# Attention products moved to even slots and input loads spaced out, in a fused attention and gated-MLP kernel

## The chip, the cores and the metric

One core of a Trainium2 chip. The metric is the device time of one launch in microseconds; a ratio is the mean time of one kernel's runs over the mean of the other's runs of the same rounds, so it is not quite the ratio of the medians quoted beside it. Each job runs the kernel before on the same chip beside the new ones.

## The reference, cut to what matters

```python
batch, n_heads, seq, head_dim = (8, 8, 576, 64)          # fp32 q, k, v

def _attn_ref(q, k, v, tau):
    scores = scale * np.matmul(q, k.transpose(0, 1, 3, 2))
    thresh = np.max(scores, axis=-1, keepdims=True) - tau
    scores = np.where(scores >= thresh, scores, -1000000000.0)
    attn = np.exp(scores - np.max(scores, axis=-1, keepdims=True))
    attn = attn / (np.sum(attn, axis=-1, keepdims=True) + 1e-09)
    return np.matmul(attn, v)

def _moe_ref(x, w_in, w_out):                            # x: 4608 x 512, w_in: 512 x 2048
    h = x @ w_in
    return ((h * np.clip(h + 3.0, 0.0, 6.0) / 6.0) @ w_out)
```

The heads of one image (batch entry) are put side by side to make the rows of `x`.

## The kernel before: the parts that matter here

The loop has 144 slots, nine per "quad" (four heads of one image, two pairs). A slot handles 128 query rows of two heads: score matmuls, the maximum on VectorE, mask and exp on ScalarE, the normalisation on GpSimd (L319), then a DMA transpose of the bf16 row, 128 x 1152 (L327), issued from SyncE. Slots 0 to 3 of a quad are its first pair, 4 to 7 its second, slot 8 is the remainder (64 rows of each of the four heads). Once a pair's rows are transposed, the attention product (`av_main`, L343) multiplies them by v; `av_rest` does the remainder. When an image is complete, its gate/up products (`mm1`, L378) are put on a list that gives one item to a slot, and its output products (`mm2`, L412) on another that gives two parts to an even slot. What is left of both lists is done behind the loop, in the tail. Four buffers hold normalised rows until their transposes have read them. From slot 22 on, rows are normalised, and their transposes issued, two at a time in odd slots. Inputs are loaded as fp32; from image 2 on q and k are loaded in 32-column blocks (four DMAs per group), and VectorE transposes the 32x32 blocks.

```python
    nat_pool = ctx.enter_context(tc.tile_pool(name="nat", bufs=3))
    v_pool = ...; qk_pool = ...; s_pool = ...          # cut
    pn_pool = ctx.enter_context(tc.tile_pool(name="pn", bufs=4))
    # ... cut ...
        def blocks_q(n, a, j):
            c = 32 * (2 * a + j)
            nc.sync.dma_start(out=nq[c:c + 32, n * S:(n + 1) * S].rearrange("p (k d) -> p k d", d=32),
                              in_=q[b, 4 * g + 2 * n + a, :, 32 * j:32 * j + 32].rearrange("(k r) d -> r k d", r=32))

        # blocks_k: the same for k; load_k(n) and load_q(n) issue four of them for the heads 2n and 2n+1 ... cut ...

        def rest():
            for dst, src in ((kr[:], k), (nq[:, 1024:1152], q))[0:2 if b < NB else 1]:
                for n in range(2):
                    nc.sync.dma_start(out=dst[64 * n:64 * n + 64, :].rearrange("p (h d) -> p h d", h=2),
                                      in_=src[b, 4 * g + 2 * n:4 * g + 2 * n + 2, 512:S, :].rearrange("h p d -> p h d"))

        for n in range(2):
            loads.append(lambda n=n: load_k(n))
            loads.append(lambda n=n: load_q(n))
            if n == 0:
                loads.append(rest)

    def sm_norm(sl):
        sl.pn = pn = pn_pool.tile([P, 2, S], BF16, tag="pn", name="pn")
        for i in range(2):
            nc.gpsimd.tensor_scalar(out=pn[:, i, :], in0=sl.s[:, i, :], scalar1=sl.rinv[:, i:i + 1], scalar2=1.0,
                                    op0=Alu.mult, op1=Alu.mult)
        if sl.slot < 8:
            pair, t = 2 * sl.quad + sl.slot // 4, sl.slot % 4
            sl.dst = pts[pair][:, :, t * P:(t + 1) * P]
        else:
            sl.dst = ptr[sl.quad][:, :, :]
        if not sl.on_chip:
            nc.sync.dma_start_transpose(out=sl.dst, in_=pn[:].rearrange("p a b -> p (a b)"))

    def av_main(pair):
        b, hp = divmod(pair, NPAIR)
        if hp == 0:
            xT[b] = x_pool.tile([P, KI, 512], BF16, tag="xT", name="xT")
        pb = bank()
        av(pb, pair, pts[pair], slice(0, 512))
        return lambda: nc.vector.tensor_copy(out=xT[b][:, hp, :], in_=pb)

    for n, sl in enumerate(queue):
        quad, slot = sl.quad, sl.slot
        b, g = divmod(quad, 2)
        now = n
        # ... cut: allocation, load_quad(quad + 2) at slot 0 of a quad (quad 5's at slot 4 of quad 3, n = 31), load_v(b + 1) at slot 0 of an odd quad ...
        # ... cut: exp of the slot before, scores' maximum of the slot after ...
        if todo1:
            item, then = todo1.pop(0)
            h = mm1(item)
            r = mm1_relu(h, on_act=even)
            mm1_gate(item, h, r)
            todo2.extend(then)
        copies = pe_transpose(queue[n - 2]) if n > 1 and queue[n - 2].on_chip else None
        if prev is not None and n < N1:
            sm_recip(prev)
        if copies:
            copies()
        for _ in range(2 if n % 2 == 0 and todo2 else 0):
            bb, mt, part = todo2.pop(0)
            mm2_part(bb, mt, part)
        for i in range(2):
            sm_mask(sl, i)
        if slot == 3 and quad > 0:
            waiting.append(av_main(2 * quad - 1))
        elif slot == 4 and quad > 0:
            waiting.append(av_rest(quad - 1))
            if quad % 2 == 0:
                todo1.extend(moe_of(quad // 2 - 1))
        if slot == 8:
            waiting.append(av_main(2 * quad))
        # ... cut: output of mm2; copies out of PSUM, put off by one slot in even slots ...
        evict = []
        for job, of in turns.get(n, ()):
            if job == "k":
                evict.append(transpose_k(of))
            elif job == "q":
                if of // 2 not in qkT:
                    alloc_qk(of // 2)
                evict.append(transpose_q(of))
            else:
                (last_keys if even else evict).append(transpose_rest(of, of_k=of > 0))
        # ... cut: scores of later slots (two slots' worth in odd slots) ...
        if prev is not None:
            ready.append(prev)
        if not even:
            for old in ready:
                sm_norm(old)
            ready = []
        flush()
        if n == 0:
            start(loads, 2)
        elif n not in (4, 12, 15, 18, 21) and not 23 < n < 34:
            start(loads, 1)
        if n < 4 or 15 < n < 20 or n > 33:
            start(vcasts, 1)
        else:
            start(casts, 2 if n in (5, 8, 11, 14) or 21 < n < 28 else 1)
        prev = sl
```

All DMA issues above, except those of v, which GpSimd issues, stand in SyncE's one queue, in the order of the program.

Of the kernel before, what the change touches and what calls it, by code (L numbers as in the profile page):

```python
# [20 lines left out]
def kernel(  # L21
# [17 lines left out]
    NQUAD = B * H // 4  # L39
    NSLOT = 9  # L40
    NB = 2
# [34 lines left out]
    loads = []  # L76
# [5 lines left out]
    def load_quad(quad):  # L82
        b, g = divmod(quad, 2)
        nat[quad] = (nat_pool.tile([P, 1152], F32, tag="nq", name="nq"),
                     nat_pool.tile([P, 4, 4, D], F32, tag="km", name="km"),
                     nat_pool.tile([P, 2 * D], F32, tag="kr", name="kr"))
        nq, km, kr = nat[quad]

        def main(dst, src, h, order, by=nc.sync):
            by.dma_start(out=dst[:, :, h, :], in_=src[b, 4 * g + h, 0:512, :].rearrange(order, t=4))  # L90
# [6 lines that stand above are left out]
        def blocks_k(n, a, j):  # L97
            c = 32 * (2 * a + j)
            nc.sync.dma_start(
                out=km[c:c + 32].rearrange("p t h d -> p (t h d)")[:, n * 512:(n + 1) * 512].rearrange(  # L100
                    "p (t m d) -> p t m d", t=4, d=32),
                in_=k[b, 4 * g + 2 * n + a, 0:512, 32 * j:32 * j + 32].rearrange("(m r t) d -> r t m d", r=32, t=4))

        def load_k(n):
            if b < NB:
                for a in range(2):
                    main(km, k, 2 * n + a, "(p t) d -> p t d")
            else:
                for a in range(2):
                    for j in range(2):  # L110
                        blocks_k(n, a, j)

        def load_q(n):
            if b < NB:
                for a in range(2):
                    main(nq[:, 0:1024].rearrange("p (t h d) -> p t h d", h=4, t=4), q, 2 * n + a, "(t p) d -> p t d",
                         by=nc.scalar if quad == n == 0 else nc.sync)
            else:
                for a in range(2):
                    for j in range(2):  # L120
                        blocks_q(n, a, j)
# [4 lines that stand above are left out]
                    nc.sync.dma_start(out=dst[64 * n:64 * n + 64, :].rearrange("p (h d) -> p h d", h=2),  # L126
                                      in_=src[b, 4 * g + 2 * n:4 * g + 2 * n + 2, 512:S, :].rearrange("h p d -> p h d"))

        for n in range(2):
            loads.append(lambda n=n: load_k(n))  # L130
            loads.append(lambda n=n: load_q(n))
            if n == 0:
                loads.append(rest)

    def load_v(b):
        vm = v_pool.tile([P, H, 4 * D], BF16, tag="vm", name="vm")
# [72 lines left out]
    def bank():  # L209
        nonlocal turn  # L210
        turn += 1
        return ps[:, (2, 5)[turn % 2], :]
# [135 lines left out]
# [8 lines that stand above are left out]
    def av_rest(quad):  # L356
# [3 lines that stand above are left out]
            av(pb[:, n * 64:(n + 1) * 64], 2 * quad + n, ptr[quad], slice(n * 64, (n + 1) * 64))  # L360
        if b % 2 == 0 and g == 0:
            xR[b // 2] = x_pool.tile([P, KI, P], BF16, tag="xR", name="xR")
        o0 = 64 * (b % 2)
        return lambda: nc.vector.tensor_copy(out=xR[b // 2][:, 2 * g:2 * g + 2, o0:o0 + 64],
                                             in_=pb[:, 0:P].rearrange("p (a b) -> p a b", a=2))
# [61 lines left out]
    todo1 = []  # L427
# [52 lines left out]
    def turn_at(n, job, of):  # L480
        turns.setdefault(n, []).append((job, of))

    for quad in range(1, NQUAD):
        n0 = quad * NSLOT
        first_odd = n0 - 9 + quad % 2
        for i, (job, of) in enumerate((("q", 2 * quad), ("k", 2 * quad), ("rest", quad),
                                       ("q", 2 * quad + 1), ("k", 2 * quad + 1))):
            turn_at(n0 + (-5, -4, -3, 0, 1)[i] if quad < 3 else first_odd + 2 * i - (job == "rest"), job, of)

    prev = None  # L490
    ready = []
    last_keys = []
    part = 0
    waiting = []
# [4 lines that stand above are left out]
        if slot in (0, 4):  # L499
            pts[2 * quad + slot // 4] = pt_pool.tile([P, 9, 512], BF16, tag="pT", name="pT")  # L500
        if slot == 8:
            ptr[quad] = ptr_pool.tile([P, 9, P], BF16, tag="pR", name="pR")
        for ahead in {0: (1, 2), 9: (3,), 16: (4,)}.get(n, (quad + 2,) if quad > 2 and slot == (4 if quad == 3 else 0) else ()):
            if ahead < NQUAD:
                load_quad(ahead)
        if slot == 0 and g == 1 and b + 1 < B:
            load_v(b + 1)
        for copy in last_keys:
            copy()
        last_keys = []  # L510
        if prev is not None:
            for i in range(2):
                sm_exp(prev, i)
        if n + 1 < len(queue):
            sm_max(queue[n + 1])
        even = n >= N1 and n % 2 == 0
        for old in ready:
            sm_recip(old)
        for copy in waiting:
            copy()  # L520
        waiting = []
# [14 lines that stand above are left out]
            mm2_part(bb, mt, part)  # L536
        for i in range(2):
            sm_mask(sl, i)
        if slot == 3 and quad > 0:
            waiting.append(av_main(2 * quad - 1))  # L540
        elif slot == 4 and quad > 0:
            waiting.append(av_rest(quad - 1))
            if quad % 2 == 0:
                todo1.extend(moe_of(quad // 2 - 1))
        if slot == 8:
            waiting.append(av_main(2 * quad))
        if part == 3:
            waiting.append(lambda tile=(bb, mt): late.extend(mm2_out(*tile, on_act=False)))
            part = 0
        if n < N1 or n % 2:  # L550
            for copy in waiting:
                copy()
            waiting = []
# [10 lines that stand above are left out]
        if n >= N1 and not even:  # L564
            sm_recip(prev)
        for out_of_psum in evict:
            if out_of_psum:
                out_of_psum()
        if n == 0:
            warm_up(8)  # L570
        if n <= N1:
            scores(n + 2)
        elif n % 2:
            for m in (n + 3, n + 2):
                if m < len(queue):
                    scores(m)
        if n < 8:
            warm_up(6)
# [6 lines that stand above are left out]
        flush()  # L585
        if n == 0:
            start(loads, 2)
        elif n not in (4, 12, 15, 18, 21) and not 23 < n < 34:
            start(loads, 1)
        if n < 4 or 15 < n < 20 or n > 33:  # L590
            start(vcasts, 1)
# [3 lines that stand above are left out]
# [80 lines left out]
```

## Time and profile before

| | |
|---|---|
| time, median of 3 runs | 563.53 us |
| profiled span | 562.4 us |
| PE / ScalarE / VectorE / GpSimd busy | 93% / 81% / 78% / 49% |
| from the start of slot 36 to that of slot 54 (quads 4 and 5) | 73.5 us |
| an undisturbed pair of quads (10 and 11) | 61.2 us |
| last masks to the end (tail) | 61.5 us |

A stretch is cut at the start of the first mask (a ScalarE instruction of L306, two a slot) of a quad's first slot. The lines that carry this, and how to read them, stand in the prediction.

### The profile page before, as it was taken

How to read it: one execution, taken by the hardware profiler on the slowest of the kernel's cores; microseconds unless marked ns; L12 is line 12 of the kernel's file. 1: busy time of each engine (PE TensorE's matmuls, PEld its weight loads, DVE VectorE, ACT ScalarE, POOL GpSimd, SP SyncE). 2: the span in 40 equal slices, each digit the busy share in tenths (PEclk: the TensorE clock that was granted, in tenths of full speed). 3: DMA queues.
4: the chain of work that ended last, by engine and by line, in shares of the span. 5: the costliest groups of instructions: out<-in, count | busy, mean ns of one | idle time of the engine just before them, and what ended most of it. 6: DMA issues, size and time to landing. Idle time of an engine off the chain costs nothing.

```text
span 562.4 us, 11583 instructions
## 1 busy us (share of the span) xinstructions
PE 520.9 (93%) x3823; PEld 323.4 (58%) x3865; DVE 439.0 (78%) x1093; ACT 455.5 (81%) x983; POOL 278.2 (49%) x502
## 2 busy tenths in 40 slices
PE   8999988997975899999999899999999999999996
PEld 6765555664543565666556565666555566664662
DVE  3888878895894798989898698988898889872540
ACT  3999979997884799899898699898898899891540
POOL 1788877564444444644465344745465454550000
PEclk9999999998997999999999899999999999999999
DMA  5899999878899878999889979999889966662302
GB/s 121 135 163 151 164 132 182 139 108 158 146 148 175 141 144 138 158 156 178 144 160 179 171 118 163 145 153 167 147 163 176 170 105 119 110 120 82 76 20 75
DMA packets 316589, 78.74 MB, mean 140 GB/s; under 512 B 299504, under 2 KB 312048, under 8 KB 316528
## 3 DMA queue, kind: packets, MB, share of 16 engines
q1 hardware_dynamic: 297920, 68.69, 69.0%
q0 software_dynamic: 17408, 8.92, 13.7%
q8 instruction: 30, 0.49, 0.4%
q10 hardware_dynamic: 1200, 0.39, 0.3%
q14 instruction: 31, 0.25, 0.2%
HBM read 36.70 MB, written 9.44 MB: 82 GB/s over the span
## 4 chain that ended last, share of the span: by engine, by line
PE 52%; ACT 9%; DMA 6%; DVE 4%; issue 3%; POOL 2%; SPq 1%; DVEq 0%; POOLq 0%; ACTq 0%
PE ps L284 17%; PE ps L412 15%; PE ps L378 13%; DMA pT<-pn 6%; PE ps L343 5%; ACT s L311 4%; ACT s L306 3%; PE ps L373 2%; POOL pn L319 1%; ACT r L386 1%; DVE s L299 1%; PE ps L346 1%; DVE g L401 1%; ACT kT L219 1%; DMA nq<-in_q_dram 0%
## 5 line engine op out<-in xcount | busy, mean ns | idle before, releaser
L319 POOL TENSOR_SCALAR pn<-s,rinv 128x576 bf16<-128x576 f32 x288 | 211.1, 745 | 83.9 <-issue 46.1
L299 DVE TENSOR_SCALAR_CACHE_REDUCE s<-ps 128x576 f32<-128x576 f32 x288 | 205.8, 752 | 40.0 <-PE ps L284 19.8
L306 ACT ACTIVATE s<-s,bias 128x576 f32<-128x576 f32 x288 | 205.8, 763 | 9.2 <-POOL bias L302 8.9
L311 ACT ACTIVATE s<-s 128x576 f32<-128x576 f32 x288 | 192.4, 670 | 0.3
L284 PE MATMUL ps<-kT,qT 64*128 64x384 f32 (+7 forms) x1280 | 186.5, 425 | 3.4 <-DVE s L299 1.6
L284 PEld LDWEIGHTS ps<-kT,qT 64*128 64x128 f32 (+1 forms) x1280 | 117.6, 178 | 60.0 <-issue 17.2
L378 PE MATMUL ps<-xT,w_in_sb 128*128 128x256 bf16 x1024 | 131.2, 274 | 6.7 <-DVE g L401 6.0
L412 PE MATMUL ps<-w_out_sb,g 128*128 128x512 bf16 x540 | 127.3, 379 | 1.9 <-issue 0.3
L378 PEld LDWEIGHTS <-w_in_sb 128*128 128x128 bf16 x1024 | 95.9, 98 | 49.4 <-issue 33.1
L401 DVE SCALAR_TENSOR_TENSOR g<-r,ps 128x512 bf16<-128x512 f32 x128 | 87.9, 688 | 19.8 <-ACT r L386 17.1
L302 POOL TENSOR_SCALAR bias<-m 128x2 f32<-128x2 f32 x144 | 27.1, 188 | 141.6 <-DVE rinv L314 103.8
L386 ACT ACTIVATE r<-ps,three 128x512 f32<-128x512 f32 x84 | 57.5, 687 | 41.0 <-PE ps L378 31.3
L412 PEld LDWEIGHTS <-g 128*128 128x128 bf16 x576 | 56.2, 98 | 57.8 <-issue 0.7
L311 ACT ACTIVATION_READ_ACCUMULATOR s<-s 128x1 f32 x288 | 54.4, 189 | 0.0
L343 PE MATMUL ps<-pT,vm 128*64 128x512 bf16 x256 | 34.6, 392 | 18.7 <-DMA pT<-pn 13.9
L388 DVE TENSOR_SCALAR r<-ps 128x512 f32<-128x512 f32 x60 | 40.7, 679 | 5.0 <-PE ps L378 3.5
L343 PEld LDWEIGHTS <-vm 128*64 128x64 bf16 x512 | 18.5, 111 | 39.2 <-issue 25.3
L420 DVE TENSOR_SCALAR osb<-ps 128x512 f32<-128x512 f32 x31 | 21.0, 677 | 24.4 <-PE ps L412 24.4
L354 DVE CAST xT<-ps 128x512 bf16<-128x512 f32 x32 | 22.0, 688 | 11.6 <-PE ps L346 10.5
L219 ACT COPY kT<-ps 64x128 f32<-64x128 f32 (+1 forms) x28 | 7.9, 282 | 23.6 <-PE ps L254 17.6
L299 DVE DVE_READ_ACCUMULATOR s<-ps 128x1 f32 x288 | 24.0, 83 | 0.0
L314 DVE RECIPROCAL rinv<-rsum 128x2 f32<-128x2 f32 x144 | 21.4, 149 | 1.4 <-ACT s L311 1.4
(56 smaller groups left out, 243.8 us busy)
## 6 DMA issues: line engine op xcount, KB each, us to landing
out_dram<-osb SPq DMA_DIRECT2D x31, 256.0 KB, 2.5
nq<-in_q_dram SPq DMA_DIRECT2D x96, 72.0 KB, 2.7
km<-in_k_dram SPq DMA_DIRECT2D x96, 64.0 KB, 2.9
vm<-in_v_dram POOLq DMA_DIRECT2D x16, 256.0 KB, 5.9
km<-in_k_dram SPq DMA_DIRECT2D x16, 128.0 KB, 3.4
w_in_sb<-in_moe_w_in_dram POOLq DMA_DIRECT2D x16, 128.0 KB, 4.6
w_out_sb<-in_moe_w_out_dram POOLq DMA_DIRECT2D x16, 128.0 KB, 4.1
pT<-pn SPq DMA_TRANSPOSE x117, 3.6
```

What stands on the lines that cost most here:

```text
L284: nc.tensor.matmul(ps_flat[rows, c0:c0 + w], qT_of(pair)[a * 64:(a + 1) * 64, q0:q0 + rows.stop - rows.start], kT_of(pair)[a * 64:(a + 1) ...
L299: nc.vector.tensor_scalar(out=sl.s[:, i, :], in0=ps_flat[:, c0:c0 + S], scalar1=1.0, scalar2=None, op0=Alu.mult, op1=Alu.max, accum_out=sl ...
L302: nc.gpsimd.tensor_scalar(out=sl.bias[:], in0=sl.m[:], scalar1=-scale, scalar2=tau, op0=Alu.mult, op1=Alu.add)
L306: nc.scalar.activation(out=s, in_=s, func=Act.Prelu, bias=sl.bias[:, i:i + 1], scale=scale, alpha=REJECT)
L311: nc.scalar.activation(out=s, in_=s, func=Act.Exp, accum_out=sl.rsum[:, i:i + 1])
L319: nc.gpsimd.tensor_scalar(out=pn[:, i, :], in0=sl.s[:, i, :], scalar1=sl.rinv[:, i:i + 1], scalar2=1.0, op0=Alu.mult, op1=Alu.mult)
L343: nc.tensor.matmul(pb[a * 64:(a + 1) * 64, :], vm[:, 2 * hp + a, c * D:(c + 1) * D], pT[:, 5 * a + c, cols], start=(c == 0), stop=False)
L378: nc.tensor.matmul(ps[:, hb, n * 256:(n + 1) * 256], w_in_sb[:, ki, (ni + n) * P:(ni + n + 1) * P], xT[b][:, ki, c0:c0 + 256], start=(ki = ...
L386: nc.scalar.activation(out=r, in_=hps, func=Act.Relu, bias=three[:])
L388: nc.vector.tensor_scalar(out=r, in0=hps, scalar1=3.0, scalar2=0.0, op0=Alu.add, op1=Alu.max)
L401: nc.vector.scalar_tensor_tensor(out=out, in0=r, scalar=6.0, in1=hps, op0=Alu.min, op1=Alu.mult)
L412: nc.tensor.matmul(o_ps[0], gbuf[:, ni, mt * P:(mt + 1) * P], w_out_sb[:, ni, :], start=(ni == 0), stop=(ni == NI - 1))
```

## The change

Its intent: let no attention product wait for its transposed rows, by giving it one or two more slots, and let no product stand in an odd slot, where the score matmuls are; and space the q and k loads, which share SyncE's queue with the transposes. Nothing is computed or moved that was not before.

```diff
--- before.py
+++ after.py
@@ -126,11 +126,14 @@
                     nc.sync.dma_start(out=dst[64 * n:64 * n + 64, :].rearrange("p (h d) -> p h d", h=2),
                                       in_=src[b, 4 * g + 2 * n:4 * g + 2 * n + 2, 512:S, :].rearrange("h p d -> p h d"))
 
-        for n in range(2):
-            loads.append(lambda n=n: load_k(n))
-            loads.append(lambda n=n: load_q(n))
-            if n == 0:
-                loads.append(rest)
+        def both():
+            rest()
+            load_k(1)
+
+        if b < NB:
+            loads.extend((lambda: load_k(0), lambda: load_q(0), rest, lambda: load_k(1), lambda: load_q(1)))
+        else:
+            loads.extend((lambda: load_k(0), lambda: load_q(0), both, lambda: load_q(1)))
 
     def load_v(b):
         vm = v_pool.tile([P, H, 4 * D], BF16, tag="vm", name="vm")
@@ -486,6 +489,12 @@
         for i, (job, of) in enumerate((("q", 2 * quad), ("k", 2 * quad), ("rest", quad),
                                        ("q", 2 * quad + 1), ("k", 2 * quad + 1))):
             turn_at(n0 + (-5, -4, -3, 0, 1)[i] if quad < 3 else first_odd + 2 * i - (job == "rest"), job, of)
+
+    products = {}
+    for quad in range(NQUAD):
+        at = (8, 12, 13) if quad < 2 or quad == NQUAD - 1 else (9, 13, 15) if quad % 2 else (8, 12, 14)
+        for job, of, after in zip(("main", "main", "rest"), (2 * quad, 2 * quad + 1, quad), at):
+            products.setdefault(quad * NSLOT + after, []).append((job, of))
 
     prev = None
     ready = []
@@ -536,14 +545,10 @@
             mm2_part(bb, mt, part)
         for i in range(2):
             sm_mask(sl, i)
-        if slot == 3 and quad > 0:
-            waiting.append(av_main(2 * quad - 1))
-        elif slot == 4 and quad > 0:
-            waiting.append(av_rest(quad - 1))
-            if quad % 2 == 0:
-                todo1.extend(moe_of(quad // 2 - 1))
-        if slot == 8:
-            waiting.append(av_main(2 * quad))
+        for job, of in products.get(n, ()):
+            waiting.append(av_rest(of) if job == "rest" else av_main(of))
+            if job == "rest" and of % 2:
+                todo1.extend(moe_of(of // 2))
         if part == 3:
             waiting.append(lambda tile=(bb, mt): late.extend(mm2_out(*tile, on_act=False)))
             part = 0
@@ -585,7 +590,7 @@
         flush()
         if n == 0:
             start(loads, 2)
-        elif n not in (4, 12, 15, 18, 21) and not 23 < n < 34:
+        elif n not in (4, 12, 15, 18, 21) and not 23 < n < 33 and (n < 37 or n % 2 == 0):
             start(loads, 1)
         if n < 4 or 15 < n < 20 or n > 33:
             start(vcasts, 1)
```

In later slots a quad's five groups of loads become four, one in each even slot, instead of five in five successive slots. Products of odd quads go from slots 8, 12, 13 (counted from the quad's own start) to 9, 13, 15; of even quads only the remainder moves, from 13 to 14.

## The prediction

> **What bounds the kernel now.** I read the page, then the waits of TensorE, then busy time by stretch. The loop runs 144 steps ("slots"), nine a quad (four heads); slots are told apart below by their number n, and the stretches are cut at the start of each quad's masks (L306). The page first:
>
> ```profile
> PE 520.9 (93%) x3823; PEld 323.4 (58%) x3865; DVE 439.0 (78%) x1093; ACT 455.5 (81%) x983; POOL 278.2 (49%) x502
> ...
> PEclk9999999998997999999999899999999999999999
> ```
>
> TensorE is busy 93% of 562.4 us, and the granted clock dips in slices 10, 13 and 23. Where is the other 7%? Quads 4 and 5 are the first two rows below, then two ordinary pairs of quads:
>
> ```profile
> 124.30:157.30 33.00, 28.69 (x192) 17.25 (x194) 24.15 (x65) 26.76 (x61) 15.23 (x30) 0.95 0.84 151
> 157.30:197.80 40.50, 28.25 (x209) 17.24 (x209) 28.05 (x69) 27.99 (x63) 18.79 (x32) 0.92 1.00 155
> ...
> 258.60:287.50 28.90, 28.38 (x207) 16.89 (x209) 25.85 (x66) 27.28 (x61) 13.76 (x27) 1.00 0.90 163
> 287.50:322.70 35.20, 32.98 (x231) 19.98 (x234) 28.52 (x70) 28.01 (x63) 18.84 (x32) 0.95 0.96 166
> 322.70:351.50 28.80, 28.39 (x217) 17.59 (x218) 25.76 (x66) 27.36 (x62) 13.79 (x27) 1.00 0.87 142
> 351.50:383.90 32.40, 31.41 (x239) 19.80 (x241) 28.99 (x71) 27.96 (x62) 18.80 (x32) 1.00 0.94 148
> ```
>
> Columns: length, busy PE, PEld, DVE, ACT, POOL, granted clock, DMA share, GB/s. An undisturbed pair (the last two rows) takes 61.2 us with PE busy 59.8: PE-bound, nothing to win. Quads 4 and 5 take 73.5 us with PE busy only 56.9: at least 12 us are lost there. Quads 8 and 9 take 64.1, some 3 us too long. What PE waits for in quads 4 and 5:
>
> ```profile
> PE ps L343 <- DMA pT<-pn: 8.8, 2, 6.2
> PE ps L343 <- DVE s L299: 3.8, 1, 3.8
> PE ps L373 <- DVE go L401: 1.9, 1, 1.9
> PE ps L378 <- DVE g L401: 1.5, 1, 1.5
> ```
>
> The first wait is attention product (L343) on the DMA transposes of the softmax rows. The second, at 131.4 us, has a DMA behind it too: VectorE stood 4.51 us before a 32x32 transpose of q whose load had not landed (VectorE's groups, nq). Why transposes are late is in the queue of SyncE:
>
> ```profile
> 154.50 1.34 SPq L126 DMA_DIRECT2D kr<-in_k_dram  x2
> 155.94 1.27 SPq L403 DMA_TRANSPOSE g<-go  x1
> 157.25 3.58 SPq L99 DMA_DIRECT2D km<-in_k_dram  x4
> 160.94 2.75 SPq L327 DMA_TRANSPOSE pT<-pn  x2
> 163.74 3.14 SPq L94 DMA_DIRECT2D nq<-in_q_dram  x4
> 166.98 3.68 SPq L327 DMA_TRANSPOSE pT<-pn  x1
> 170.75 1.52 SPq L327 DMA_TRANSPOSE pR<-pn  x1
> ```
>
> It issues without a break. The pair of transposes at 160.94 belongs to slot 43, whose masks ran at 151.2: the queue is some 9 us behind. The product at n=48 needs the row transposed at 166.98, landing at 173.54; PE idles 6.17 us. The same shape gives 1.89 us at 316.0 (product at n=89, transposes issued 8 us after their slot).
>
> **The skill.** (1) "TensorE: Matmul & The Clock Gate", Part 1: idleness throttles the array to half clock for a window. The trace agrees: 16 score matmuls take 2.21 us normally, 4.20 us after the idle time at 136.5 and 3.90 at 317.2. (2) "DMA: Bandwidth & Descriptors", Issuing engines are not separate DMA queues: all issuers share the same 16 engines. Agrees: the transposes of p landed 3.2 us (median) after issue in 101 to 117 us, but 6.6 us in 160 to 175, while GpSimd's two v loads of 256 KB were under way. (3) "Perfetto Trace Analysis", Per-instruction lifecycle, HWDGE: the row of a DMA instruction is its issue alone, not the transfer. Agrees: transposes issue in 1.3 us and land after 3.2. So issue time, which occupies SyncE, and landing are counted apart here. (4) Same page, Identifying the Most-Contended Engine: matmul occupancy is a poor measure of headroom. I therefore take the best undisturbed quads of this trace as the floor, not PE's share.
>
> **The change, part by part.** No arithmetic, buffer or DMA is added or removed; the order of instructions shows equal counts on PE and SyncE (260 rows there). Three things move.
>
> *Loads.* Before, a quad's five groups (k, q, rest, k, q) go out in five successive slots: between two pairs of transposes (odd slots) SyncE issues up to k and q, 2.66 + 2.2 = 4.9 us (four DMAs of about 0.66 and 0.55 each), with the transposes 2 x 1.33 and an output 0.6: 8.2 us. Two ordinary slots last 61.2/9 = 6.8 us, so a backlog builds twice a quad and drains in the last four slots. After, one group goes per two slots, the largest (rest and k) 1.3 + 2.7 = 4.0: at most 7.3 us, typically 5.5. Also, quad 5's loads start at n=33 rather than 34. Its first q is then ahead of slot 35's transposes rather than behind them; those took 5.35 us to issue, so q lands about 5 us earlier and the 4.51 us of VectorE and 3.75 us of PE go. Between the transposes of slot 37 and those of slot 45 the queue before issued the second k and q of quad 5 and all of quad 6; after, that k and q are already out by slot 36: 2.66 + 2.2 = 4.9 us off a lateness of 9.
>
> *Products.* Those of odd quads move from slots 8, 12, 13 to 9, 13, 15 (counted from the quad's start); of even quads only the remainder moves, 13 to 14. The one at n=89 goes to 90: a slot, 3.4 us, plus earlier transposes, against a wait of 1.89: gone, with its clock dip. But the product at n=48 stays at 48. It gains by the queue alone: 4.9 us off, 6.17 needed; POOL then also gets its pn buffers back earlier (it waited 4.3 us for that). I leave 1 to 2 us of this wait standing.
>
> *MoE.* The list of gate/up products of an image is filled with its remainder, now two slots later from the second image on. Walking through the loop, n=41 and 42 lose their item, and everything after is two slots later: 7 items rather than 5 and 10 output parts rather than 8 are left for the end. Cost there: 2 x 0.95 (eight matmuls of L378; the tail does 104 in 11.52 us, so 0.89 to 0.98) + 2 x 4 x 0.216 (L412, 62 in 13.76 us with fill) = 1.9 + 1.7 = 3.6 us. PE is full in the tail, so all of it counts; it covers the 1.27 us that the last product but one waits at 507.32. Net +2.3.
>
> The sum over the span. Quads 4 and 5: the throttled windows inflate PE's 56.9 by about 3.5 (1.9 + 1.7 us), and 3.6 move to the tail: some 50 us of PE work is left, so ScalarE (26.76 + 27.99 = 54.8) becomes the bound. In even quads it is busy 27.3 of 28.8 us, so the floor is 54.8 x 28.8/27.3 = 57.8; with 2 us of waits left, 60. That is -13.5. Quads 8 and 9: 64.1 to 61.2, -2.9. Quads 12 and 13: 61.8 to 61.2, -0.6. Tail: +2.3. Together -14.7: span 547.7, and the timed run is about 1 us above the span (563.53 against 562.4): 548.8. Such sums seldom come in full, so I add a little: **549.5 us**, 2.5% faster.
>
> **Rivals.** (a) *The late stretch stays DMA-bound.* The bytes are unchanged, DMA share is 1.00 in quad 5, and the v loads still fall on slots 45 to 48, just where n=48 needs its row. Then half of the 13.5 stays: about 556. Against: the ordinary odd quads carry the same v loads at share 0.94 to 1.00 and PE does not wait at their fourth slot; only quad 5 begins with a backlog. (b) *PE is the bound and the move only pushes work to the end.* For: 59.8 of 61.2 in ordinary pairs. Then +2.3 alone: 566. Against: 73.5 us in quads 4 and 5 is no PE-bound time. (c) *Loads become the wait:* spread over eight slots, the last q and k of a quad land later and VectorE, in order, waits for them as it did at 133 us. Against: the last group goes out at slot 6 or 7 and is transposed seven to nine slots later. Worth a few us at most, where quads 5 and 6 start: 552. (d) *Even slots get too heavy:* an even slot holds gate/up 1.0, output 1.7 and product 1.25, about 4 us, an odd one 3.4; VectorE's copy of the product waits for the next slot. This balances rather than hurts, as odd slots with a product had 4.7; but it could delay scores by some tenths a quad: +2 us.
>
> **Range and chances.** If (a) holds in full, 556 to 559; if all waits vanish, 545. Eight in ten: 543 to 559. The 2% line is at 552.3, nearer to my figure than half the uncertainty: faster 0.63, same 0.35, slower 0.02.
>
> **What would show it.** Right: quads 4 and 5 take 58 to 62 us together; no gap over 2 us before L343; slices 10, 13 and 23 at full clock; SyncE no more than about 4 us behind its slot at the 48th; the tail from the last masks about 2 us longer than 61. Wrong: the gap before the product at n=48 is still over 4 us (a); ordinary pairs over 62 us (d); VectorE waiting on nq or km (c); pairs unchanged at 61 and quads 4 and 5 above 68, with the tail longer, would bring it to "same".

## The result, and the profile after

The changed kernel takes 555.52 us (median of 4; 555.29 to 556.12) beside 563.83 for the one before. The ratio is 0.9857, with a 95% interval of 0.9833 to 0.9881: 1.4% less, under the 2% from which a change counts as faster, and 6 us more than the 549.5 predicted. The page of the changed kernel (busy time by engine; TensorE's granted clock in 40 slices):

```profile
PE 519.7 (94%) x3824; PEld 319.1 (58%) x3865; DVE 439.2 (79%) x1091; ACT 456.8 (82%) x985; POOL 278.3 (50%) x502
...
PEclk9999999998997999999999999999999999999999
```

The work is the same. The clock dip in slice 23 is gone; those in slices 10 and 13 are not. By stretch (quads 4 and 5, then 8 and 9, then the tail; columns as in the prediction):

```profile
122.50:154.00 31.50, 28.07 (x187) 14.28 (x188) 23.17 (x61) 26.07 (x59) 15.52 (x30) 0.95 0.94 164
154.00:191.20 37.20, 26.28 (x190) 16.47 (x191) 27.17 (x68) 28.03 (x64) 18.96 (x33) 0.91 0.97 157
...
251.50:282.00 30.50, 29.39 (x219) 16.49 (x220) 26.82 (x67) 27.38 (x62) 13.72 (x27) 1.00 0.92 160
282.00:312.80 30.80, 30.45 (x222) 18.81 (x223) 28.11 (x69) 27.94 (x62) 18.34 (x32) 1.00 0.87 148
...
490.30:554.00 63.70, 58.82 (x383) 34.97 (x384) 23.90 (x39) 24.31 (x41) 2.93 (x4) 1.00 0.25 68
```

Side by side, us (the last column is an experiment told below):

| stretch | before | predicted | after | early loads |
|---|---|---|---|---|
| start to quad 3 | 93.0 | 93.0 | 92.1 | 92.2 |
| quad 3 | 31.3 | 31.3 | 30.4 | 30.4 |
| quads 4 and 5 | 73.5 | 60 | 68.7 | 60.3 |
| quads 6 and 7 | 60.8 | 60.8 | 60.3 | 60.4 |
| quads 8 and 9 | 64.1 | 61.2 | 61.3 | 61.3 |
| quads 10 and 11 | 61.2 | 61.2 | 60.4 | 60.4 |
| quads 12 and 13 | 61.8 | 61.2 | 61.3 | 61.3 |
| quad 14, quad 15 to its last masks | 55.2 | 55.2 | 55.8 | 55.8 |
| tail | 61.5 | 63.8 | 63.7 | 63.7 |
| span | 562.4 | 547.7 | 554.0 | 545.7 |

All but one row came within 1 us of what was worked out: quads 4 and 5 gained 4.8 us, not 13.5. What TensorE waited for there (waits of PE in quads 4 and 5; total, times, longest):

```profile
PE ps L346 <- DMA pT<-pn: 6.5, 1, 6.5
PE ps L381 <- DVE g L404: 3.7, 3, 1.9
PE ps L287 <- DVE s L302: 2.2, 1, 2.2
```

L346 is the attention product (L343 before). The wait at slot 48 is as long as it was, 6.46 us against 6.17. SyncE's queue, followed by the normalisation on GpSimd of the row in question:

```profile
152.29 1.34 SPq L126 DMA_DIRECT2D kr<-in_k_dram  x2
153.68 2.66 SPq L99 DMA_DIRECT2D km<-in_k_dram  x4
156.44 2.80 SPq L330 DMA_TRANSPOSE pT<-pn  x2
159.34 1.29 SPq L406 DMA_TRANSPOSE g<-go  x1
160.68 4.55 SPq L94 DMA_DIRECT2D nq<-in_q_dram  x4
165.33 2.48 SPq L330 DMA_TRANSPOSE pT<-pn  x1
```

```profile
153.90 1.47 POOL L322 TENSOR_SCALAR pn<-s,rinv 128x576 bf16<-128x576 f32 x2
...
159.09 0.80 POOL L143 DMA_DIRECT2D vm<-in_v_dram  x1
...
160.21 0.79 POOL L143 DMA_DIRECT2D vm<-in_v_dram  x1
```

The row of slot 43 (told by the remainder's transpose, pR, right behind it in the queue) is normalised at 155.4 us and its transpose issued at 165.33: 10.0 us in the queue. (Rows are named here by the slot that handles them; the prediction names transposes by the odd slot in which they are issued, so the pair that it says belongs to slot 43 holds the rows of slots 41 and 42.) Before, the same row waited 8.4 us (normalised at 158.6, issued at 166.98). The queue had not become shorter at this point at all. Meanwhile GpSimd issues the two v loads of image 3, at 159.09 and 160.21, and the four q loads behind them take 4.55 us to issue instead of 2.2.

### The profile page after: what moved, and what is told of

It reads as the page before. It is cut to its first block, busy times and chain, and to the rows that moved or that the text cites.

```text
span 554.0 us, 11585 instructions
## 1 busy us (share of the span) xinstructions
PE 519.7 (94%) x3824; PEld 319.1 (58%) x3865; DVE 439.2 (79%) x1091; ACT 456.8 (82%) x985; POOL 278.3 (50%) x502
## 4 chain that ended last, share of the span: by engine, by line
PE 67%; DVE 7%; ACT 6%; issue 2%; DMA 2%; SPq 1%; POOL 1%; DVEq 0%; POOLq 0%; ACTq 0%
PE ps L287 20%; PE ps L415 19%; PE ps L381 18%; PE ps L346 5%; DVE s L302 3%; ACT s L314 3%; PE ps L376 2%; ACT s L309 2%; DVE g L404 2%; ACT r L389 1%; PE ps L349 1%; DMA pT<-pn 1%; DMA nq<-in_q_dram 1%; DVE r L391 1%; PE ps L257 1%
## 5 line engine op out<-in xcount | busy, mean ns | idle before, releaser
L287 PE MATMUL ps<-kT,qT 64*128 64x384 f32 (+7 forms) x1280 | 184.4, 421 | 5.3 <-DVE s L302 3.9
L287 PEld LDWEIGHTS ps<-kT,qT 64*128 64x128 f32 (+1 forms) x1280 | 116.0, 176 | 60.9 <-issue 18.3
L381 PEld LDWEIGHTS <-w_in_sb 128*128 128x128 bf16 x1024 | 94.6, 98 | 47.3 <-issue 33.6
L346 PE MATMUL ps<-pT,vm 128*64 128x512 bf16 x256 | 34.6, 393 | 7.6 <-DMA pT<-pn 6.5
L346 PEld LDWEIGHTS <-vm 128*64 128x64 bf16 x512 | 18.1, 111 | 33.0 <-issue 17.7
L421 ACT ACTIVATE osb<-ps 128x512 f32<-128x512 f32 x5 | 3.0, 597 | 28.1 <-PE ps L415 21.9
```

The source lines that it names most:

```text
L287: nc.tensor.matmul(ps_flat[rows, c0:c0 + w], qT_of(pair)[a * 64:(a + 1) * 64, q0:q0 + rows.stop - rows.start], kT_of(pair)[a * 64:(a + 1) ...
L346: nc.tensor.matmul(pb[a * 64:(a + 1) * 64, :], vm[:, 2 * hp + a, c * D:(c + 1) * D], pT[:, 5 * a + c, cols], start=(c == 0), stop=False)
L381: nc.tensor.matmul(ps[:, hb, n * 256:(n + 1) * 256], w_in_sb[:, ki, (ni + n) * P:(ni + n + 1) * P], xT[b][:, ki, c0:c0 + 256], start=(ki = ...
```

## The experiments

Theories. **A:** SyncE's queue holds the transposes back; the loads ahead of them decide. **B:** the DMA engines do; v's loads slow whatever is under way beside them. **P:** the products' move, not the loads, carries the gain. **C:** the two slots of MoE work that the change pushes behind the loop cost it what the tail grew by. All kernels start from the changed one unless said otherwise, and all were timed in 3 rounds.

### Each half alone

Loads alone: the products' slots back to `at = (8, 12, 13)` for every quad.

```diff
-        at = (8, 12, 13) if quad < 2 or quad == NQUAD - 1 else (9, 13, 15) if quad % 2 else (8, 12, 14)
+        at = (8, 12, 13)
```

> The changed loads with the products where they stood before (slots 8, 12, 13 of every quad). Theory A (the late transposes come from loads ahead of them in SyncE's queue, so the gain is the loads'): the wait of 1.89 us at slot 89 is gone or under 0.5, quads 8 and 9 take 61 to 62 us against 64.1, quads 4 and 5 take 67 to 70, the tail stays at 61.5, so about 553 to 555 us, at or under the full change. Theory P (the gain comes from moving the products to even slots): 560 us or more, and quads 8 and 9 stay near 64.

Measured: 553.08 us (550.97 to 553.99), ratio 0.9798 (0.9759 to 0.9836). Quads 8 and 9 take 60.5 us and PE does not wait before the product at slot 89; quads 4 and 5 take 69.8, with a wait of 6.63 us at slot 48; the tail is 60.8.

Products alone: the loads as before.

```diff
-        if b < NB:
-            loads.extend((lambda: load_k(0), lambda: load_q(0), rest, lambda: load_k(1), lambda: load_q(1)))
-        else:
-            loads.extend((lambda: load_k(0), lambda: load_q(0), both, lambda: load_q(1)))
+        loads.extend((lambda: load_k(0), lambda: load_q(0), rest, lambda: load_k(1), lambda: load_q(1)))
...
-        elif n not in (4, 12, 15, 18, 21) and not 23 < n < 33 and (n < 37 or n % 2 == 0):
+        elif n not in (4, 12, 15, 18, 21) and not 23 < n < 34:
```

> The changed products with the loads as before. Theory A: SyncE stays late in quads 4 and 5 (72 to 74 us), the product at slot 90 waits less than 0.5 us because it stands a slot later, ordinary pairs go from 61.2 to about 60.4 us, and the tail is 2.2 us longer: 560 to 563 us. Theory P: quads 4 and 5 fall to 68 to 70 here too and the time is about 556.

Measured: 559.31 us (558.20 to 560.91), ratio 0.9916 (0.9877 to 0.9954). Quads 4 and 5 take 69.7 us, which I had expected of theory P (68 to 70) and not of A (72 to 74); quads 8 and 9 take 61.3, and the tail is 63.7.

What follows: the loads alone give at least as much as both halves; the intervals of 0.9798 and 0.9857 overlap by a hair, so a small loss by the products isn't shown. P falls for the change as it stands (with earlier loads, below, the products' slots do matter). Either half removes the wait in quads 8 and 9. In quads 4 and 5 each alone gives about 4 us and both together no more than 4.8, so something else sets the time there.

### Queue or engines, at slot 48

Queue: nothing is loaded in slot 44, which puts the last q of quad 6 behind the transpose that slot 48 needs.

```diff
-        elif n not in (4, 12, 15, 18, 21) and not 23 < n < 33 and (n < 37 or n % 2 == 0):
+        elif n not in (4, 12, 15, 18, 21, 44) and not 23 < n < 33 and (n < 37 or n % 2 == 0):
```

> The full change, but nothing is loaded in slot 44, so the last q of quad 6 goes out in slot 46, behind the transposes that the product at slot 48 needs, and later loads of quads 6 to 8 follow two slots later. Theory A (SyncE's queue holds these transposes): their issue comes about 4 us earlier than the last one's landing at 170.5 us implies, the 6.46 us wait before the product falls to 2 to 3 us, and the time to 551 to 553 us. Theory B (the DMA engines, busy with v, slow them whenever they are issued): the transposes start earlier but land late, the wait stays over 4 us, 554 to 556 us.

Measured: 554.89 us (553.66 to 555.13), ratio 0.9831 (0.9797 to 0.9864). The wait at slot 48 is 5.38 us. SyncE's queue of this run, then the transposes to `pT` issued between 160 and 170 us with their time from issue to landing:

```profile
158.69 1.30 SPq L406 DMA_TRANSPOSE g<-go  x1
160.09 1.64 SPq L330 DMA_TRANSPOSE pT<-pn  x1
```

```profile
L330 SPq DMA_TRANSPOSE pT<-pn x1: 1637/1637/1637, 160.1 to 160.1; - x1
...
DMA to landing us min/median/max: 9.4/9.4/9.4
```

The transpose was issued 5.2 us earlier than in the full change (160.09 against 165.33), as A asks, and took 9.4 us to land instead of 5.1, as B asks: it landed at 169.5, only 1.0 us earlier. The v loads were issued at 159.28 and 160.39 in this run, on both sides of it.

Engines: the v of image 3 is loaded six slots later, the q loads stay ahead.

```diff
-        if n < 4 or 15 < n < 20 or n > 33:
+        if n < 4 or 15 < n < 20 or n > 33 and not 44 < n < 51:
             start(vcasts, 1)
```

> The full change, but the v of image 3 is loaded in slots 51 to 54 instead of 45 to 48. Theory B: the transposes for slot 48 land 3.3 us after issue instead of 5.1, the q loads ahead of them issue in 2.2 us instead of 4.6, the wait falls from 6.46 to about 2 us, 551 to 552 us. Theory A: the transposes still stand behind the loads; only the issue of the q loads shortens, the wait stays over 4 us, 554 us or more.

Measured: 552.56 us (552.19 to 552.76), ratio 0.9793 (0.9755 to 0.9831). The wait at slot 48 is 2.06 us, quads 4 and 5 take 63.4. The same two views:

```profile
161.14 3.20 SPq L94 DMA_DIRECT2D nq<-in_q_dram  x4
164.44 1.28 SPq L330 DMA_TRANSPOSE pT<-pn  x1
```

```profile
DMA to landing us min/median/max: 3.3/3.3/3.3
```

The row still stands 9.2 us in the queue (10.0 in the full change), but lands in 3.3 us. The q loads ahead of it took 3.20 us to issue, not the 2.2 expected. At slot 48 B explains most of the wait, and A's part is that the queue was late enough to put the transpose into v's window.

Both together (slot 44 without a load, v of image 3 later):

> The full change with both: v of image 3 in slots 51 to 54 and nothing loaded in slot 44. With v out of the way the transposes that slot 48 needs were issued at 164.4 us, behind the q loads (161.1 to 164.3), and landed in 3.3 us. Theory A+B (the remaining 2.06 us wait is the queue's part): they issue 3 us earlier, the wait is under 0.5 us, 551 to 552 us. Rival (queue order never mattered, only the engines): still about 2 us, 552.5 us.

Measured: 553.99 us median, but of two kinds: 551.29 and 551.51, and 556.46 and 557.85; ratio 0.9859 (0.9801 to 0.9916). The profiled run (551.51) waits 0.84 us at slot 48, but 1.98 us elsewhere, at 228.2 us. Why two of the four runs were 5 us longer is open; their mean granted clock was 0.990, against 0.996 and 0.997 in the others, but no profile of them was taken. The run decides nothing about the time. For slot 48 it shows A's own part: with v away, issuing the transpose at 159.99 us rather than at 164.44 took the wait from 2.06 to 0.84 us.

### Where the lateness comes from

In the changed kernel the rows of slots 33 to 38 already stand 5.0 to 9.6 us between normalisation and issue (1.8 to 4.3 before, for those that stand at all), while those of 29 to 32 stand 0.0. It begins where quad 5's loads go out: `n < 37 or n % 2 == 0` lets them go in four successive slots, 33 to 36, just when v of image 2 is loaded (34 to 37). So I let them begin as soon as the quad is put on the list, in slot 31, before v:

```diff
-        elif n not in (4, 12, 15, 18, 21) and not 23 < n < 33 and (n < 37 or n % 2 == 0):
+        elif n not in (4, 12, 15, 18, 21) and not 23 < n < 31 and (n < 37 or n % 2 == 0):
```

> The full change, but quad 5's loads start two slots earlier (slot 31 rather than 33). Theory: the gap of 2.25 us at 132.9 us and the clock dip behind it come from the q load of quad 5 landing late (VectorE waited 1.93 us for it), so both go and quads 3 and 4 take 59.5 to 60.5 us together rather than 61.9: 553 to 554 us. Rival: the loads now collide with SyncE's transposes of quad 3 and the gap moves: no change.

Measured: 547.82 us (547.53 to 549.95), ratio 0.9736 (0.9712 to 0.9759): 2.6% less, which neither half had given, from one number. I had expected 1.5 to 2.5 us; it gave over 7. Quads 4 and 5, and SyncE's queue around the row of slot 43:

```profile
122.60:150.70 28.10, 24.98 (x176) 12.71 (x178) 22.76 (x60) 26.02 (x60) 15.62 (x30) 1.00 0.97 168
150.70:182.90 32.20, 27.23 (x203) 17.98 (x202) 27.49 (x68) 27.91 (x63) 19.01 (x33) 0.95 1.10 168
```

```profile
152.50 2.72 SPq L330 DMA_TRANSPOSE pT<-pn  x2
155.31 1.28 SPq L406 DMA_TRANSPOSE g<-go  x1
156.69 1.34 SPq L330 DMA_TRANSPOSE pT<-pn  x1
158.55 1.27 SPq L330 DMA_TRANSPOSE pR<-pn  x1
```

The stretch takes 60.3 us, and ScalarE is the busiest engine in it (26.02 + 27.91 of 60.3). PE no longer waits for a transpose at slot 48, but it waits 1.97 us before the product of slot 44. The profile puts this wait down to VectorE, yet the last row of that product, issued at 146.86, landed 3.4 us later, at 150.26, and the product began at 150.45: part of the wait for transposes has moved four slots forward. The row of slot 43 stood 4.6 us in the queue instead of 10.0 and was issued at 156.69, ahead of the v loads (158.47 and 159.59); it landed in 3.3 us. The remainder's transpose just behind it, issued at 158.55, took 7.2. VectorE's wait of 1.93 us for q, and PE's 2.25 us behind it at 132.9 us, are gone too.

The early loads did not put the queue on time: the rows of slots 33 to 42 still stand 5.2 to 8.2 us in it. What changed for slot 48 is what stands directly ahead of the row of slot 43. Quad 6's last q now goes out in slot 42, so only an output transpose (`g<-go`) is in between. In the run with q later that place was empty too, and the row stood 4.4 us in the queue there, about as long as here, yet PE waited 5.38 us. The difference is when GpSimd issues v, which it does right behind the normalisation of the next row. First q later, then the early loads:

```profile
157.87 1.47 POOL L322 TENSOR_SCALAR pn<-s,rinv 128x576 bf16<-128x576 f32 x2 [2.22 <-issue]
159.28 0.80 POOL L143 DMA_DIRECT2D vm<-in_v_dram  x1
```

```profile
157.05 1.47 POOL L322 TENSOR_SCALAR pn<-s,rinv 128x576 bf16<-128x576 f32 x2 [5.01 <-DVE rinv L317]
158.47 0.80 POOL L143 DMA_DIRECT2D vm<-in_v_dram  x1
```

With q later the transpose went out 0.8 us behind v's first load, with the early loads 1.8 us ahead of it, and part of this lead was not planned: GpSimd stood 5.01 us before that normalisation (2.22 with q later). In the other three runs with early loads and v in its place the transpose leads too, by 0.5 to 3.1 us. So A and B are one: what counts is whether the queue lets the transpose out before v's loads begin.

With v of image 3 later as well:

> The full change with quad 5's loads from slot 31 and v of image 3 in slots 51 to 54. If the early loads have already taken the backlog away, v has nothing left to delay: 547 to 548.5 us, no gain over 547.8. If v still costs by itself: 545 to 546 us.

Measured: 548.23 us (546.97 to 549.87), ratio 0.9726 (0.9699 to 0.9753): no gain over 547.82. The transpose for slot 48 already went out ahead of v, so nothing was left to gain there; the product of slot 44, at 152.5 us, waits 2.95 us for its rows (1.97 with v in its place).

### What the MoE work in the tail costs

First try, remainders of odd quads at 13, in one slot with the second product (`(9, 13, 15)` becomes `(9, 13, 13)`):

> The full change, but the remainders of odd quads stand at slot 13 as before (behind the second product of the same slot) instead of 15, so the gate/up list is filled as early as in the kernel before. Theory C (the two slots of MoE work that the change pushes behind the loop are paid in the tail): the tail from the last masks falls from 63.7 to about 61 us, the rest of the loop stays, 552.5 to 553.5 us. Rival (the work pushed out was hidden or is paid in the loop instead): no change, 555 to 556 us.

Measured: 552.86 us (551.82 to 556.21), ratio 0.9827 (0.9791 to 0.9864), and a **wrong result** (relative error 1.53). By the program's order, this slot then holds three users of two PSUM banks (product, remainder, and the transposes of a later quad's remaining rows of k), and the copy out of the first comes a slot later; that this is what went wrong was not tested. Its tail is 61.1 us, but its quads 4 and 5 take 69.4, and a wrong kernel proves little. Three correct ones follow, all with the early loads. Products as before, `at = (8, 12, 13)`:

> The changed loads with quad 5's from slot 31, products as before. Theory L (the loads carry the gain, the products' move costs 2 to 3 us in the tail and gives nothing back once the loads are spread): tail 61 us, quads 4 and 5 near 61, about 544.5 to 546 us, 2 us under the full change with early loads (547.8). Rival P (in the clean stretch the products need their later slots): L346 waits over 2 us for transposes at slots 39 or 48 and the time is 548 us or more.

Measured: 548.09 us (547.22 to 548.46), ratio 0.9720 (0.9700 to 0.9739). Tail 60.8, quads 4 and 5 62.3, quad 3 31.3. The rival came true: PE waits 3.68 us before the second product of quad 3, at slot 39:

```profile
135.46 1.05 PE L346 MATMUL ps<-pT,vm 128*64 128x512 bf16 x8 [3.68 <-issue]
```

The transposes of its last two rows were issued at 129.4 and 130.8 us and took 3.5 and 4.5 us to land, so the wait ends just as the second has landed (135.3, if the longer time is its own). In the early loads with the products moved, this product stands at slot 40 and does not wait.

Second products and remainders of odd quads earlier, `(9, 13, 15)` to `(9, 11, 13)`:

> The full change with quad 5's loads from slot 31, and the second product of odd quads at slot 11, the remainder at 13, all still even slots; the gate/up list is then filled two slots earlier, as in the kernel before. Theory C (tail): last masks to end 61 to 61.5 us instead of 63.7, and if slot 11 is late enough for its transposes the time is 545 to 546 us. Rival: the product at slot 11 waits over 1 us a pair of quads for transposes and eats it: 547.5 us or more.

Measured: 547.69 us (547.03 to 548.62), ratio 0.9716 (0.9695 to 0.9737). Tail 60.8, quads 4 and 5 64.2. The same product, here at slot 38, waits 3.35 us.

Products moved only up to quad 5, `quad == NQUAD - 1` to `quad > 5`:

> The full change with quad 5's loads from slot 31, and the products of quads 6 to 15 where they stood before, so that the MoE list catches up at quad 7. Theory C: tail 61 to 61.5 us, ordinary pairs of quads 60.6 to 60.8, 545 to 546 us. Rival (the later products help the ordinary pairs): pairs over 61.2 and no gain, 547.5 us or more.

Measured: 549.55 us (547.13 to 550.87), ratio 0.9744 (0.9706 to 0.9782). Tail 63.7: my expectation was wrong in its premise. The list gives one item a slot; the two more slots (41 and 42) in which it is empty cannot be made up later, wherever the remainders of later quads stand.

So the tail is 2.8 us shorter wherever the first lists are filled two slots earlier, as C says, and yet the time does not fall: quads 3 to 5 take that much longer. For the early loads with and without the products' move, quads 3 to 5 and the tail sum to the same 154.4 us (90.7 + 63.7 and 93.6 + 60.8, to rounding). In two other pairs of profiles with and without the move the sums differ by 0.8 us (161.5 without, 162.3 with: loads alone against the full change) and 1.2 us (156.4 and 155.2: early loads with v later). C holds for the tail and falls for the whole. With the early loads two things differ in quads 3 to 5: without the move the two MoE items are done there, and the second product of quad 3 waits 3.0 to 3.7 us for its rows. How much each makes was not separated, and each kernel has one profile.

### An attempt to beat both

The early loads, v of image 3 later, and the products as before, `at = (8, 12, 13)`:

> The changed loads alone (products as before), v of image 3 later, and quad 5's loads from slot 31: an attempt to beat both. If the three effects add: 553.1 less 4 to 5 us for v, less 1 to 3 us for the earlier loads: 545 to 548 us, quads 4 and 5 at 60 to 63 us, tail near 61. If the products' move is needed once the stretch is clean: 550 us or more, with waits of L346 on transposes again.

Measured: 547.90 us (545.89 to 550.37), ratio 0.9731 (0.9696 to 0.9766). Quads 4 and 5 take 64.6 us in its profile, not the 60 to 63 expected; PE waits 3.02 us before the second product of quad 3. The six versions with the early loads lie between 547.7 and 549.6 us with overlapping intervals; which is the best isn't settled. The simplest is the changed kernel with 33 made 31.

## Why the prediction was right and wrong

The time lies in the range (543 to 559 us), but not because the sum held: it came where rival (a) had put it, at "about 556", and the change was in the class "same", which had 0.35, and not in "faster", which had 0.63. Two of the signs of being wrong appeared: the wait at slot 48 is over 4 us (6.46), and quads 4 and 5 take over 68 us (68.7).

- **PE bounds the ordinary quads: the trace agrees.** In quads 6 and 7 PE is busy 60.0 of 60.3 us after, and ordinary pairs take 60.3 to 61.3 us with the products in quite other slots.
- **Quads 8 and 9 lose their wait and clock dip, 2.9 us: right,** 2.8. That I gave the product's own slot a part in it was unneeded: the loads alone do it too, and so does the products' move.
- **Quads 12 and 13 give 0.6 us: right,** 0.5.
- **The tail grows by 2.3 us: right in size,** 2.2. But I booked it as a cost beside the rest. In three pairs of profiles with and without the products' move, what the tail gains in time the stretch of quads 3 to 5 loses, to within 1.2 us.
- **Quads 4 and 5 come down to 60 us: wrong by 8.7 us, and this is the whole miss.** The step that failed is "4.9 us off a lateness of 9". It took two groups of loads off the queue between slots 37 and 45 and did not follow where they went: into slots 33 to 36, four groups in a row, beside v. The queue was then later from slot 33 on (5.0 us and more), and the row of slot 43 waited 10.0 us rather than 8.4. Nor did the queue recover: from 129.6 to 172.7 us SyncE issues without a break, and the 6.8 us that I allowed it for two slots held a supply of 5.5 to 7.3 us of issues only, with nothing for what was already waiting. Nearly half of the 10.0 us is quad 6's q group (4.55 us), which still stood directly ahead: without it the row stood 4.4 us (q later) and 4.6 us (early loads), though the rows before it stayed late in both.
- **The floor of 58 to 60 us itself was nearly reached:** the early loads take 60.3 us, with ScalarE busy 53.9 and PE 52.2. That ScalarE is the bound isn't shown: PE still waited 1.97 us at slot 44, and the granted clock was 0.95 in quad 5.
- **"q lands about 5 us earlier and VectorE's wait goes": half right.** The wait fell from 4.51 to 1.93 us; the q group stood ahead of the transposes but its loads, 4.7 us from issue to landing, were beside v's.
- **Rival (a), the stretch stays DMA-bound, came true** as far as v goes: later v takes most of the wait. What I said against it (ordinary quads carry the same v loads) was sound for them and hid the point: there, after the change, the transpose of the same slot's row is issued 1.5 to 3.8 us before v's first load (quads 6, 8, 10 and 12), here the late queue carries it to 6.2 us behind. Rivals (b), (c) and (d) didn't show: no ordinary pair became slower (only quads 14 and 15 did, by 0.6 us), and no q or k load arrived late except the one named.

## What to carry to other kernels

Where transposes and loads share one issuing queue, look at how long each transpose stands between the end of the work that feeds it and its own issue, and at what stands directly ahead of the one that stalls. Here the lateness began ten slots before the stalling row, but moving one group of loads from just ahead of that row took it from 10.0 to 4.4 us while the rows before it stayed late. A transfer that is late is worse than its lateness if it falls beside a large load of another queue (9.4 us to land instead of 3.3), so count who else is issuing in the window it lands in. And when work is moved from one stretch into another, measure the sum of both: here a tail longer by 2.8 us cost nothing on the whole.

## What the Trainium skill lacked or had wrong

- "DMA: Bandwidth & Descriptors", Issuing engines are not separate DMA queues, calls the sequencer's time to start a DMA "usually small relative to the DMA itself". Here a transpose of a 128 x 1152 bf16 row issues in 1.3 us and lands 3.3 us after the start of its issue, and beside v's loads (in the run with q later) issue took up to 4.1 us and landing up to 9.4. SyncE issued without a break from 129.6 to 172.7 us after the change, so its issue time was not a detail here.
- "TensorE: Matmul & The Clock Gate", Why this matters for your kernels, asks for no idle gaps above about 3 us. A single gap of 1.89 us (at 316.0 us before) and one of 2.25 us (at 132.9 us after) were each followed by 16 score matmuls in 3.90 and 4.03 us instead of 2.21; gaps of 1.87 us elsewhere (159.5 us after) were not. Shorter gaps than the page names can thus cost 1.7 us more than themselves, though not always.
